# A conditioned attention and token-mixing block on one core: the same operations in a new issue order, with other engines for some norms and evacuations

## The chip, the cores and the metric

One core of a Trainium2 chip runs the whole program. The metric is the device time of one execution in microseconds (us). The core has five engines that run their own instruction lists in order and wait for each other through semaphores: TensorE (PE; its weight loads are listed apart as PEld), VectorE (DVE), ScalarE (ACT), GpSimd (POOL) and SyncE (SP). SP does no arithmetic here; it issues nearly all transfers (DMAs), one after the other.

## What is computed

```
h = layernorm(x) * (1 + ca) + sa                      # x: 2048 x 512
x = x + ga * A(h, wqkv, wo)
h = layernorm(x) * (1 + cb) + sb
x = x + gb * B(h, w1, b1, w2, b2)                     # sa..gb: six rows of silu(c) @ w_mod

A: q, k, v = h @ wqkv   (32 heads of 16)
   each position attends to 8 positions: itself and 2, 4, .. 14 back
   softmax over the 8, weighted sum of v, then @ wo
B: h = layernorm(h);  u = gelu(h^T @ w1 + b1)         # over the 2048 positions: 512 x 1792
   y = u @ w2 + b2;   return y^T
```

All inputs and the output are bf16. There are three layernorms per position: two on x and one inside B.

## The kernel before

The 2048 positions are 16 tiles of 128 (`st` 0 to 15), in five chunks of 2, 4, 4, 4 and 2 tiles. A chunk has 256 or 512 columns once it is transposed.

Each chunk goes through the same steps; their names are the tokens of the issue order:

- `ln1s`, `rstd1`, `nb1`, `n1`: the first layernorm. The statistics of a tile are a pair of VectorE instructions (for tiles 10 to 13 two ACT passes and `ln1v`), `rstd` two tiny ACT functions, `nb` one tiny VectorE instruction for the tiles of a group, and `n1_<tile>` the norm itself, one 128x512 instruction. A norm can run on ACT, VectorE or GpSimd.
- `tr`/`hT` (chunks 0 and 1: transposes on TensorE, copied out of PSUM) or `xt` (chunks 2 to 4: transposing DMAs).
- `wsc`: the three weight blocks of the projection, scaled once by 1 + ca, in four pieces each.
- `qkv<chunk>_<t><j>`, `ev...`: projections for q, k and v (t = 0, 1, 2) and their evacuation from PSUM with a bias.
- `qk<chunk>_<i>`, `red`: VectorE multiplies q with the 8 shifted copies of k, for a quarter of the head's lanes at a time, into one of four `big` buffers (a "full product" has 128x4096 elements, a "half" one, in chunks 0 and 4, 128x2048); TensorE sums it over lanes into the logits in `psL`.
- `max`, `sub`, `exp`, `esum`, `rcp`, `smB`: the softmax, going between VectorE, TensorE and ACT.
- `a2`, `vd`: DMAs that lay the weights and the shifted v out for the next step. `pv`, `pvacc`, `oev`: the weighted sum, with four products per chunk on VectorE like those of `qk`, summed on TensorE.
- `wo`, `x1`, `ln2q`: output projection, residual, and the sums for the second layernorm. `ln2m`, `rstd2`, `nb2`, `n2`: that layernorm. `aff`: times 1 + cb plus sb, two VectorE instructions. `ln3s`, `rstd3`, `nb3`, `h3`: the third layernorm.

The first product of B (`mlp1`) sums over positions. It is cut in three sweeps, so that its first part can run when only the first tiles are normed: `mlp1_<sweep>_<f>_<tile>` are 128x512 matmuls from that tile on; `park` puts a partial sum into SBUF, `inj` puts it back by an identity matmul, `padd` adds it on VectorE; `gelu` follows on ACT. The second product (`mlp2_<tile>`) has 14 matmuls per output tile; `fin` (two VectorE instructions) finishes a tile and `st_out` stores it. The last tile is done in pieces of 256, 128 and 128 columns. Loads of weights are `ld_...`, on SP's queue in the order of their tokens.

Nothing on the device schedules. The string `ORDER` (L182 to L238) lists all operations; `_Graph.schedule` (L85) takes them in that order, gives each its buffer from a pool (six PSUM banks `ps`, four `big`, five `vd`) and each engine issues its own in that sequence. A suffix selects the engine where several are possible (`:a` ACT, `:d` VectorE, `:p` GpSimd), and `:q` makes a matmul four 32-column ones (`mm`, L511). For the norms the engine comes from the tuple `NE` (L265: one string per layernorm, one letter per tile), and `ln_norm` (L404) hands only that one on. Where a group's norms are all on VectorE, `nb` is left out (L397).

Idle stretches of TensorE are filled by matmuls of the identity with itself: `fill:2:70` and `fill:4:16` (70 and 16, `fill_fn`, L517) and four `warm` of 9 (L522). They read `ident`, which GpSimd builds (`mk_ident`, L463).

All instructions are recorded by one helper, so each line of the profile says L133; operations are told apart by tile names: `psS` is a PSUM bank, `psL` the logits, `h` any of the normed tiles, `wst` streamed weights, `m` the maxima, `lsb` the softmax weights, `gT` the values after gelu or a parked partial sum.

Of the kernel before, what the change touches and what calls it, by code (L numbers as in the profile page):

```python
# [41 lines left out]
class _Graph:  # L42
# [42 lines left out]
    def schedule(self):  # L85
# [4 lines left out]
        for pos, token in enumerate(ORDER.split()):  # L90
            name, *rest = token.split(":")
            if name == "fill":
                k, n = map(int, rest)
                f = _Op(-1, [("pe", 0.06 * n, lambda k=k, n=n: self.fill_fn(k, n))], 0.0, "filler", 0)
                f.alloc = f.frees = f.behind = None
                order.append(f)
                continue
# [85 lines left out]
consts ld_x_1_2 act_table ld_x0 ld_x_1_4 ld_c ld_x_2_8 ld_x1 ident ld_x_2_6 ld_wmod1 ln1s3 halo0 ld_wqkv1 cps  # L183
ln1s2 warm2 ld_wqkv0 silu_exp ld_wmod0 ln1s0 ln1s4 ln1s1 ln1s5 rstd1_0 ld_x_4_14 nb1_0 ln1s9 rstd1_1 n1_0 n1_1
silu_dve nb1_1 ld_wqkv2 ln1s8 fill:2:70 tr0_0 n1_2 n1_4 modcols1 ln1s7 hT0_3:a n1_5 n1_3 ld_x_3_10 hT0_2:d a1col
hT0_0:a fill:4:16 tr1_2 wsc1_2:d ld_b1 hT0_1:a wsc1_3:d wsc1_0:a tr1_0 wsc1_1:d ln1s6 hT1_2:a ld_wmod2 qkv0_10
ld_x_3_12 wsc0_0:d rstd1_2 wsc0_1:d qkv0_12 wsc0_2:d hT1_1:a nb1_2 n1_8 n1_9 wsc0_3:d modcols0 hT1_0:d ld_wmod3
hT1_3:a qkv0_00 sab ev0_12:d n1_6 ld_wmod4 qvb0 ln1s14 ld_wo1 qkv0_02 qvb_cp0 ln1s15 ev0_00:a wsc2_2 qvb1
wsc2_0:d qkv1_00 wsc2_3 ev0_10:a ev0_02:d ln1s10 wsc2_1:d qkv1_10 qvb_cp1 qk0_0 ev1_10:a qkv0_22 qk0_1 n1_7
qkv0_20 ln1s13 qk0_2 qkv1_02 xt6 red0_0 ev1_00:a qk0_3 red0_1 red0_2 ev0_22:a ld_wmod5 qkv1_22 qk1_0 ev0_20:a  # L190
qkv1_12 ev1_02:a vd0_1 red0_3 ev1_12:a mask qkv1_11 vd0_0 ln1s11 max0 xt8 qk1_2 qkv1_01 ev1_11:a sub0 qkv1_03
ev1_01:a xt9 exp0 qkv1_13 qk1_1 ev1_03:a xt7 esum0 ev1_13:a qkv1_20 rcp0 vd0_2 ln1s12 qkv1_21 smB0 qk1_3 a2_0_3
modcol2 rstd1_4 qkv1_23 a2_0_0 ev1_22:a a2_0_2 halo_v1:a red1_0 ev1_20:a a2_0_1 red1_1 ln1v10 ln1v12 ln1v11
ln1v13 nb1_4 red1_2 rstd1_3 n1_15 ld_wo3 red1_3 nb1_3 ld_wo2 mcols0 n1_11 n1_10 qkv2_00 max1 ev1_21:a n1_14 xt10
qkv2_02 ev2_00:a pv0_0 qkv2_10 n1_12 ld_wo0 pv0_1 qkv2_11 vd0_3 ev2_10:a ev2_02:a qkv2_12 qk2_0 n1_13 qkv2_01
xt12 ev2_12:a pvacc0_0 ev2_01:a sub1 qk2_2 xt13 qkv2_03 exp1 qkv2_13 xt11 ev2_11:a ev2_03:a qkv2_22 qk2_1
ev2_13:a esum1 ev1_23:a qkv2_21 rcp1 vd1_2 red2_0 smB1 ev2_21:a ld_b2 red2_1 qk2_3 halo_v2:a a2_1_1 red2_2
pvacc0_1 a2_1_3 qkv3_00 a2_1_2 qkv3_10 a2_1_0 pv0_2 mrowt0 vd1_1 qkv2_20 ev3_10:a pv0_3 ev3_00:a red2_3 mrows0:a
qkv2_23 ev2_20:a st_row0 max2 halo_k3:p ev2_22:a vd1_3 qkv3_11 qk3_0 xt14 qkv3_22 ev3_11:a pvacc0_2 ld_row0
pvacc0_3 sub2:q oev0_2:a vd1_0 pv1_2 qkv3_02:q exp2 qkv3_12 ev3_02:a ev2_23:a qkv3_01 pv1_3 oev0_0:a vd2_2 esum2  # L200
modcol3 xt15 rcp2 ev3_12:a woq_s qkv3_20 ev3_01:a pvacc1_3 smB2 ev3_20:a red3_0 qk3_1 ev3_22:a a2_2_0 pvacc1_2
wo1 a2_2_1 vd2_3 qkv3_13:q x1_1 a2_2_2 pv1_1 vd2_1 wo0 ev3_13:a a2_2_3 qkv4_02 ld_w1_0_512 oev1_2:a mcols1 pv1_0
ld_w1_0_0 oev1_3:a mrowt1 qkv3_03 mrows1:a x1_0 st_row1 qkv4_00 ev3_03:a vd2_0 ln2q1 qk3_2 pvacc1_0 ev4_02:a
red3_1 pvacc1_1 oev1_0:a qkv3_23:q oev1_1:a qk3_3 ev4_00:a wo3:q ln2q0 wo5:q pv2_2 qkv4_22:q x1_5 ev3_23:a wo2:q
ld_row1 ln2q5 ld_w1_0_896 ln2m0 halo_v3:a wo4:q x1_3 pv2_1 x1_2 red3_2 x1_4 red3_3 ln2q3 qkv3_21:q pv2_3 rstd2_0
qkv4_20 ln2q2 ev3_21:a ev4_22:a vd3_3 pvacc2_1 nb2_0 max3 pvacc2_2 n2_0 warm0 ln2q4 vd3_0 n2_1 ln2m2 sub3 pv2_0
pvacc2_3 oev2_2:a exp3 rstd2_2 esum3 oev2_1:a aff0 pvacc2_0 rcp3 oev2_0:a qkv4_10 oev2_3:a ln2m4 nb2_2 smB3
warm3 n2_2 ev4_10:a ln3s0 wo6 a2_3_0 n2_3 ln3s1 a2_3_1 rstd2_4 wo7 x1_6 vd3_1 aff2 rstd3_0 a2_3_2 biascols wo9:q
ev4_20:a a2_3_3 nb2_4 nb3_0 ln3s3 n2_5 n2_4 vd3_2 warm1 ln3s2 h3_1 h3_0 qkv4_12 aff4 rstd3_2 wo8 x1_7 ld_w2_0
nb3_2 ln3s5 h3_3 h3_2 ln2q6 ln3s4 mlp1_0_6_0 ev4_12:a pv3_0 mlp1_0_3_0 x1_9 rstd3_4 mlp1_0_5_0 x1_8 mlp1_0_0_0  # L210
biascols_cp:a ln2q8 nb3_4 pv3_1 halo_v4:a mlp1_0_2_0 h3_4 vd4_1 h3_5 mlp1_0_1_0 ln2q9 pv3_2 ld_w2_1 mlp1_0_2_4
vd4_2 ln2q7 mlp1_0_0_4 vd4_0 mlp1_0_3_4 park0_0:a mlp1_0_1_4 mlp1_0_5_4:q park0_1:a ln2m6 vd4_3 pv3_3 park0_2:a
pvacc3_0 pvacc3_1 oev3_0:a ld_w1_0_1152 pvacc3_2 oev3_1:a mlp1_0_4_0:q rstd2_6 oev3_2:a qk4_2 pvacc3_3 park0_3:a
mlp1_0_7_0 oev3_3:a nb2_6 qk4_1 n2_6 mlp1_0_6_4 mlp1_0_4_4 n2_8 qk4_0 wo12:q ld_w1_0_1408 n2_7 n2_9 qk4_3 wo10:q
park0_4:a aff6 x1_12 red4_0 wo13:q ld_w2_3 park0_5:a ln2q12 red4_1 red4_2 x1_10 red4_3 wo11:q max4 ln2q10 ln3s9
x1_13 sub4:q mlp1_0_8_0:q exp4 ln3s8 ln2q13 mlp1_0_11_0 esum4 ln3s7 rcp4 mlp1_0_12_0 park0_6:a ln3s6 x1_11
mlp1_0_10_0 smB4 rstd3_6 ln2m12 a2_4_2 mlp1_0_9_0 h3_7 rstd2_12 h3_6 a2_4_3 ln2q11 h3_9 mlp1_0_8_4 ln2m13 a2_4_0
nb2_12 ln2m11 n2_12 mlp1_0_7_4 a2_4_1 ln2m10 h3_8 rstd2_10 ld_w2_4 aff12 mlp1_0_9_4 rstd2_13 rstd2_11 nb2_10
ln3s12 mlp1_0_9_8 mlp1_0_7_8 n2_10 mlp1_0_8_8 nb2_13 pv4_0 park0_7:a mlp1_0_12_4 ld_w1_0_1664 park0_8:a
mlp1_0_11_4 nb2_11 pv4_2 n2_13 mlp1_0_10_4 rstd3_12 pv4_1 park0_9:a mlp1_0_12_8 n2_11 mlp1_0_10_8 pv4_3 inj1_4  # L220
mlp1_0_11_8 ld_w1_1_0 park0_10:a pvacc4_2 ld_w1_1_640 park0_11:a pvacc4_0 nb3_12 aff11 pvacc4_1 h3_12 pvacc4_3
mlp1_0_13_0 aff10 oev4_0:a oev4_2:a aff13 mlp1_0_13_4 ln3s10 wo15 ld_w2_5 ln3s13 rstd3_10 mlp1_0_13_8 wo14 x1_15
rstd3_13 park0_12:a inj1_0 nb3_13 ln2s15 mlp1_1_0_6 nb3_10 x1_14 rstd2_15 mlp1_1_4_6 park0_13:a nb2_15 ln2s14
n2_15 inj1_3 inj1_6 ld_w1_1_896 inj1_5 mlp1_1_6_6 rstd2_14 aff15 h3_10 mlp1_1_3_6 ln3s15 mlp1_1_6_10 ln3s11
mlp1_1_0_10 rstd3_15 inj1_1 mlp1_1_1_6 park1_0:a nb3_15 h3_15 n2_14 rstd3_11 aff14 mlp1_1_5_6 h3_13 ln3s14
mlp1_1_5_10 mlp1_1_1_10 inj1_2 ld_w1_2_0 mlp1_1_2_6 h3_11 rstd3_14 park1_1:a h3_14 mlp1_1_4_10 mlp1_1_3_10
mlp1_1_2_10 mlp1_1_9_10 park1_2:a ld_w1_1_1408 park1_3:d mlp1_1_7_10 padd1_9 park1_4:a park1_5:d mlp1_1_8_10
padd1_7 gelu7 mlp1_1_10_10 park1_6:a mlp1_2_2_11 ld_w1_2_640 padd1_10 mlp1_2_2_14 mlp1_2_0_11 padd2_2
mlp1_2_0_14 ld_w2_7 gelu2 mlp1_2_1_11 padd2_0 mlp1_2_1_14 gelu0 mlp1_1_12_10 padd2_1 gelu10 padd1_8 gelu1
mlp1_2_5_11 gelu8 mlp1_2_5_14 gelu9 mlp1_2_6_11 mlp1_2_3_11 padd2_6 mlp1_2_3_14 ld_w2_9 mlp1_2_4_11 padd2_3  # L230
# [11 lines left out]
def kernel(  # L242
# [10 lines left out]
    c: bass.AP,  # L253
    w_mod: bass.AP,
    out: bass.AP,
    SIZES=(2, 4, 4, 4, 2),
    MIX=((0, 7, (6, 11)), (7, 14, (10,))),
    NPRE=6,
    NBIG=4,
    NVD: int = 5,  # L260
    NHT: int = 2,
    NA2: int = 2,
    NB=2,
    NH2=2,
    NE=('PAPAAPAADAAPAAPD', 'PAPAAPAAAADAAADP', 'APPAAADDDDADAADA'),  # L265
    X1D=(14, 15),
    ESD=(4,),
    LN1A=(10, 11, 12, 13),
    LN2D=(14, 15),
    GRP=(2, 2, 4, 1, 1),  # L270
    XDMA=(2, 3, 4),
    INJ=(1,),
    WARM=4,
    VPOOL=(2, 3),
):
    nc = _OrderedNC(tc, 1)
    G = _Graph(dict(ps=6, big=NBIG, vd=NVD))
# [109 lines left out]
    def ln_rstd(l, g0, n, name, var=None, vreads=None):  # L387
# [9 lines left out]
        if vreads is None and NE[l][g0:g0 + n] == "D" * n:  # L397
            return
# [118 lines left out]
    def fill_fn(k, n):  # L517
        for _ in range(n):
            nc.tensor.matmul(psS[k][:, 0:P], lhsT=ident[:], rhs=ident[:], start=True, stop=True)
# [519 lines left out]
```

## Time and profile before

| | |
|---|---|
| median of 3 runs | 206.48 us (206.46 to 206.7) |
| span of the profiled execution, first to last instruction | 204.6 us |
| TensorE busy | 194.7 us (95%), 1655 matmuls |
| VectorE busy | 163.3 us (80%), 260 instructions |
| ACT busy | 120.6 us (59%), 283 |
| GpSimd busy | 13.0 us (6%), 36 |
| norms on ACT, 128x512 | 27, mean 0.805 us |
| norms on VectorE, 128x512 | 10, mean 0.404 us |
| norms on GpSimd, 128x512 | 11, mean 0.806 us |
| weighted products on VectorE, 128x4096 | 24, mean 2.285 us |
| moved by DMA | 35.93 MB, mean 176 GB/s |

The span is what the trace covers; 1.9 us lie around it. Busy times of engines overlap and don't add up to the span. A matmul's listed duration (379 ns for 512 columns) covers its whole way through the array; the next one starts about 213 ns later. In the lists of instructions a line reads: start, duration, engine, source line, operation, output<-input, shape, count; neighbours of the same kind are merged, with their count.

### The profile page before, as it was taken

The numbers are of one execution on the slowest core, as the hardware profiler recorded it, in microseconds if no ns is written. First come the engines' busy times: TensorE is split into PE (matmuls) and PEld (weight loads), VectorE is DVE, ScalarE is ACT, GpSimd is POOL, SyncE is SP. The second block draws the span as 40 slices with busy tenths as digits, with TensorE's granted clock in tenths as the row PEclk, the third lists the DMA queues.
The fourth block names the chain that finished last, engine by engine and source line by source line (L and its number), as shares of the span: only waits on it lengthen the run. The fifth ranks groups of instructions, "written<-read, shape, count | busy, mean of one in ns | idle before, by whom it ended". The sixth has DMA issues, their size and how long they took to land.

```text
span 204.6 us, 4223 instructions
## 1 busy us (share of the span) xinstructions
PE 194.7 (95%) x1655; PEld 103.5 (51%) x1655; DVE 163.3 (80%) x260; ACT 120.6 (59%) x283; POOL 13.0 (6%) x36
## 2 busy tenths in 40 slices
PE   3999999999999997989899999999999999999994
PEld 3988554454455553554344445444444444444453
DVE  2899999999999999999999999975473204369365
ACT  2398998994666899989898876683762000000000
POOL 4122001100000001240000000100000000000000
PEclk9999999999999999999999999999999999999999
DMA  5999494646958976194975179946990930121121
GB/s 141 330 380 348 117 239 107 161 98 201 247 186 267 308 234 251 25 272 110 289 200 115 26 157 263 288 131 200 340 304 3 232 88 16 39 77 51 51 82 51
DMA packets 55111, 35.93 MB, mean 176 GB/s; under 512 B 24628, under 2 KB 52404, under 8 KB 55092
## 3 DMA queue, kind: packets, MB, share of 16 engines
q1 hardware_dynamic: 55084, 35.67, 61.4%
q8 instruction: 13, 0.21, 0.4%
q14 instruction: 6, 0.05, 0.1%
q10 hardware_dynamic: 8, 0.00, 0.0%
HBM read 22.55 MB, written 2.10 MB: 121 GB/s over the span
## 4 chain that ended last, share of the span: by engine, by line
PE 65%; DVE 20%; issue 5%; DMA 5%; SPq 3%; ACT 2%; DVEq 0%
PE psS L133 62%; DVE big L133 9%; DVE h L133 3%; PE psL L133 3%; SPq L133 3%; DVE st L133 3%; DMA wst<-in_B_w_dram 2%; DMA xx<-in_A_x_dram 2%; ACT h L133 1%; DVE mv L133 1%; DVE m L133 1%; DVE lsb L133 1%; DVE ls L133 0%; DVE nb L133 0%; DVE woq L133 0%
## 5 line engine op out<-in xcount | busy, mean ns | idle before, releaser
L133 PE MATMUL psS<-h,wst 128*128 128x512 bf16 (+1 forms) x254 | 50.7, 379 | 1.2 <-POOL h L133 0.7
L133 PE MATMUL psS<-hT,w_qkv 128*128 128x512 bf16 (+3 forms) x312 | 46.2, 339 | 0.3 <-ACT w_qkv L133 0.3
L133 PEld LDWEIGHTS <-wst 128*128 128x128 bf16 (+1 forms) x356 | 28.7, 98 | 32.2 <-issue 3.2
L133 PEld LDWEIGHTS <-w_qkv 128*128 128x128 bf16 (+1 forms) x354 | 29.5, 111 | 21.3 <-issue 3.2
L133 DVE TENSOR_TENSOR big<-a2sb,vD 128x4096 bf16<-128x4096 bf16 (+1 forms) x20 | 36.9, 1876 | 0.0
L133 DVE TENSOR_TENSOR big<-q_sb,k_f 128x4096 bf16<-128x4096 bf16 (+1 forms) x20 | 36.3, 1857 | 0.0
L133 DVE SCALAR_TENSOR_TENSOR h<-psS,bcol,rows_bc 128x512 f32<-128x512 f32 (+2 forms) x18 | 12.4, 690 | 24.4 <-PE psS L133 24.2
L133 PE MATMUL psS<-gT,big 128*128 128x512 bf16 x112 | 24.8, 379 | 0.0
L133 PEld LDWEIGHTS <-big 128*128 128x128 bf16 x144 | 12.0, 97 | 13.2
L133 PEld LDWEIGHTS <-ident 128*128 128x128 bf16 (+1 forms) x203 | 13.9, 111 | 5.9 <-issue 2.8
L133 PE MATMUL psS<-woq,o_sb 128*32 128x512 bf16 (+1 forms) x172 | 16.6, 380 | 0.0
L133 ACT ACTIVATE h<-xx,nb,rs 128x512 bf16<-128x512 bf16 x19 | 15.0, 807 | 0.8 <-DVE nb L133 0.7
L133 DVE TENSOR_TENSOR psS<-psS,gT 128x512 f32<-128x512 f32 x14 | 9.3, 696 | 7.0 <-PE psS L133 7.0
L133 ACT ACTIVATE junk<-xx 128x512 bf16<-128x512 bf16 x22 | 13.8, 626 | 0.2
L133 POOL TENSOR_SCALAR h<-xx,rs,nb 128x512 bf16<-128x512 bf16 x9 | 7.3, 813 | 101.3 <-DVE nb L133 84.0
L133 ACT ACTIVATE lv<-mv,epscol 128x1 f32<-128x1 f32 (+2 forms) x25 | 7.3, 291 | 9.3 <-DVE mv L133 8.4
L133 DVE BATCH_NORM_STATS2 st<-xx 128x6 f32<-128x512 bf16 x14 | 9.5, 678 | 4.0 <-DMA xx<-in_A_x_dram 4.0
L133 ACT ACTIVATE gT<-psS,bcol 128x512 bf16<-128x512 f32 x14 | 8.7, 688 | 6.4 <-DVE psS L133 6.4
L133 PEld LDWEIGHTS <-group 128*32 128x32 bf16 x288 | 6.8, 96 | 10.2 <-issue 4.8
L133 DVE TENSOR_TENSOR h<-h,rows_bc 128x512 bf16<-128x512 bf16 (+2 forms) x20 | 11.5, 581 | 0.5
L133 DVE TENSOR_TENSOR h<-h,xx 128x512 bf16<-128x512 f32 (+2 forms) x18 | 11.4, 633 | 0.6
L133 ACT ACTIVATE gT<-psS 128x512 bf16<-128x512 f32 x19 | 10.8, 587 | 1.6 <-PE psS L133 1.5
(94 smaller groups left out, 220.4 us busy)
## 6 DMA issues: line engine op xcount, KB each, us to landing
vD<-v_sb SPq DMA_DIRECT2D x12, 524.5 KB, 3.8
big<-in_B_w_dram SPq DMA_DIRECT2D x4, 896.0 KB, 8.2
vD<-v_sb SPq DMA_DIRECT2D x8, 268.5 KB, 3.0
wst<-in_B_w_dram SPq DMA_DIRECT2D x3, 640.0 KB, 5.3
out_dram<-h SPq DMA_DIRECT2D x15, 128.0 KB, 1.8
xx<-in_A_x_dram SPq DMA_DIRECT2D x7, 256.0 KB, 6.1
wst<-in_B_w_dram SPq DMA_DIRECT2D x2, 800.0 KB, 4.8
gT<-in_w_mod_dram SPq DMA_DIRECT2D x3, 512.0 KB, 6.1
```

Of the source, the lines that this page charges most:

```text
L133: r = fn(*a, **k)
```

## The change

The operations are the same but for a few fills and column operations. The string `ORDER` is new as a whole. The rest of the diff, nearly complete:

```diff
         for pos, token in enumerate(ORDER.split()):
             name, *rest = token.split(":")
-            if name == "fill":
-                k, n = map(int, rest)
-                f = _Op(-1, [("pe", 0.06 * n, lambda k=k, n=n: self.fill_fn(k, n))], 0.0, "filler", 0)
...
-    NE=('PAPAAPAADAAPAAPD', 'PAPAAPAAAADAAADP', 'APPAAADDDDADAADA'),
...
-    WARM=4,
+    WARM=(9, 70, 16),
...
-        if vreads is None and NE[l][g0:g0 + n] == "D" * n:
-            return
...
-    def ln_norm(l, g0, n, st, dst, src, reads, writes, name, by_sums=False):
...
+    def ln_norm(l, g0, st, dst, src, reads, writes, name):
+        rs, nb = ln_t["rs", l], ln_t["nb", l]
+        r_, n_ = rs[:, st, 0:1], nb[:, st, 0:1]
+        G.add_any([("act", 0.8, lambda: nc.scalar.activation(dst, src, ACT.Identity, scale=r_, bias=n_)),
+                   ("dve", 0.42, lambda: nc.vector.tensor_scalar(dst, src, r_, n_, op0=ALU.mult, op1=ALU.add)),
+                   ("pool", 0.8, lambda: nc.gpsimd.tensor_scalar(dst, src, r_, n_, op0=ALU.mult, op1=ALU.add))],
+                  reads=reads + [("rs", l, g0), ("nb", l, g0)], writes=writes, name=name, locks=True)
...
-    for w_ in range(WARM):
+    for w_, n_w in enumerate(WARM):
         s_w = _Slot("ps")
 
-        def f_warm(s_w=s_w):
-            for _ in range(9):
+        def f_warm(s_w=s_w, n_w=n_w):
+            for _ in range(n_w):
                 nc.tensor.matmul(ps(s_w)[:, 0:P], lhsT=ident[:], rhs=ident[:], start=True, stop=True)
```

Every `nb` is now computed, and the engine of a norm is its suffix in `ORDER` (ACT where there is none). Two stretches of the old and the new order, at the start and (new order alone) where the third norm of tiles 4 and 5 and the second of tiles 6 and 7 stand:

```diff
-consts ld_x_1_2 act_table ld_x0 ld_x_1_4 ld_c ld_x_2_8 ld_x1 ident ld_x_2_6 ld_wmod1 ln1s3 halo0 ld_wqkv1 cps
-ln1s2 warm2 ld_wqkv0 silu_exp ld_wmod0 ln1s0 ln1s4 ln1s1 ln1s5 rstd1_0 ld_x_4_14 nb1_0 ln1s9 rstd1_1 n1_0 n1_1
-silu_dve nb1_1 ld_wqkv2 ln1s8 fill:2:70 tr0_0 n1_2 n1_4 modcols1 ln1s7 hT0_3:a n1_5 n1_3 ld_x_3_10 hT0_2:d a1col
-hT0_0:a fill:4:16 tr1_2 wsc1_2:d ld_b1 hT0_1:a wsc1_3:d wsc1_0:a tr1_0 wsc1_1:d ln1s6 hT1_2:a ld_wmod2 qkv0_10
+ld_x_1_2 ident warm1 ln1s3 ld_x0 ld_x1 ld_c ln1s0 ln1s1 ld_x_1_4 act_table ld_wqkv1 ln1s4 rstd1_0 nb1_0 n1_0:a cps
+ln1s2 ld_wmod1 ln1s5 n1_1:p tr0_0 ld_x_2_6 silu_exp silu_dve rstd1_1 hT0_2:d nb1_1 n1_4:p hT0_1:d ld_wmod0 halo0
+hT0_3:a n1_3:d ld_wqkv0 n1_5:a modcols1 a1col wsc1_2:a n1_2:d tr1_2 wsc1_1:a ld_x_2_8 hT1_3:a ld_b1 tr1_0 hT1_1:a
+wsc1_3:d hT1_0:a wsc0_1:a hT0_0:d wsc0_0:a ld_x_4_14 wsc1_0:d qkv0_10 consts ev0_10:a ln1s6 ld_wqkv2 wsc2_2 ln1s7
...
+nb3_4 a2_3_1 h3_4:p h3_5:p x1_8 mlp1_0_5_0 a2_3_0 a2_3_2 pv3_2 ln2q9 ln2q8 ln2m6 rstd2_6 vd3_1 mlp1_0_0_0
+halo_v4:a pv3_0 mlp1_0_1_4 mlp1_0_3_4 mlp1_0_0_4 nb2_6 n2_6:p park0_0:a park0_1:a n2_8:a mlp1_0_2_4 park0_2:a
+mlp1_0_4_4 mlp1_0_6_0 mlp1_0_6_4 park0_3:a pvacc3_2 n2_7:p mlp1_0_5_4 oev3_2:a pv3_1 mlp1_0_8_0 pvacc3_1
```

What the orders say by count:

| | before | after |
|---|---|---|
| norms on ACT / VectorE / GpSimd | 27 / 10 / 11 | 13 / 9 / 26 |
| n1 on GpSimd (tiles) | 0, 2, 5, 11, 14 | 1, 4, 7, 8, 9, 10, 11, 14, 15 |
| n2 on GpSimd | 0, 2, 5, 15 | 1 to 7, 9, 13, 15 |
| h3 on GpSimd | 1, 2 | 0, 3, 4, 5, 8, 9, 10 |
| weight scalings on ACT / VectorE / GpSimd | 1 / 9 / 2 | 6 / 4 / 2 |
| hT copies on VectorE | 2 of 8 | 3 of 8 |
| ev and park on VectorE | 4 | 0 |
| small halo copies on GpSimd | 1 | 3 |
| identity matmuls: ahead of the first projection / in the middle | 95 / 27 | 70 / 25 |
| mlp1 matmuls ahead of sub4 in TensorE's order | 46 | 74 |
| mlp1 and inj matmuls split in columns (:q) | 10 | 64 |

In the new order `fin14` and four stores stand ahead of the last two pieces of tile 15, whose 256 columns come earlier; `mlp2` starts with tile 7; tile 0, whose matmuls stand in three parts, comes eighth and no longer first.

## The prediction

> **What bounds the kernel now.** I read the busy rows in slices first, then the busy time by stage, then the chain of waits, and last the order of time on VectorE, GpSimd and TensorE.
>
> ```profile
> PE   3999999999999997989899999999999999999994
> DVE  2899999999999999999999999975473204369365
> POOL 4122001100000001240000000100000000000000
> ```
>
> TensorE (PE) and VectorE (DVE) are both full from the third slice to the twenty-sixth; from there on only TensorE is. GpSimd (POOL) is nearly empty. A "full" PE can hide waits, so the stages come next (us, busy time and count for PE, PEld, DVE, ACT, POOL, then granted clock, DMA share, GB/s):
>
> ```profile
> 20.00:30.00 10.00, 10.00 (x71) 5.57 (x70) 10.00 (x8) 9.57 (x23) 0.00 (x0) 1.00 0.75 197
> 80.00:90.00 10.00, 9.21 (x96) 5.46 (x95) 9.72 (x21) 9.31 (x24) 2.67 (x3) 1.00 0.50 169
> 100.00:109.20 9.20, 8.46 (x128) 3.74 (x121) 9.17 (x10) 8.52 (x21) 0.00 (x0) 1.00 0.92 246
> 144.00:201.60 57.60, 57.57 (x295) 27.50 (x293) 29.14 (x44) 7.67 (x13) 0.00 (x0) 1.00 0.39 112
> ```
>
> Up to 109 us VectorE hardly rests, while TensorE begins to have holes at 70 us. In the last 57.6 us TensorE has no hole and VectorE is half idle. The chain of waits says where the bound changes hands:
>
> ```profile
> 13.61 9.50 PE psS L133 x108
> ...
> 108.57 0.60 DVE m L133
> ...
> 112.83 88.75 PE psS L133 x465
> ...
> 201.60 0.36 DVE h L133
> ```
>
> So: the first projection starts at 13.61, VectorE leads until the last maximum of the attention logits (max4, started 108.48, 108.48 + 0.68 = 109.16 at its end), then TensorE runs straight to 201.58 and 3.0 us of tail follow. Two quantities make the time: when max4 is done, and how much TensorE work stands behind it (sub4, the matmul that waits for it, started at 109.22).
>
> **The change, step by step.** All is measured against the span of 204.6; the median of 206.48 is 1.9 above it, and I add that at the end.
>
> *Start.* The 70 fill matmuls move to the very front, GpSimd builds the identity first, and the first weight block is issued fifth on SP's queue, not eighth. DVE takes the statistics of tiles 3, 0, 1 first (0.80 each from 3.65, so 6.05), then ACT needs 0.5 for rstd and DVE 0.1 for nb: the norms of chunk 0 start at 7.0 and not 9.2. Following ACT's new list from there (silu, hT0_3, n1_5, two weight scalings at 0.70, three hT1 copies at 0.59, two more scalings, ev0_10, hT1_2, rstd, two halves of ev0_00 at 0.47), the first projection can start at 11.9 and the first attention product (qk0_0) at 17.7, not 19.48. Both are 1.7 to 1.8 earlier. If ACT, which is 89 to 96% busy here, slips, half of this is gone.
>
> *The fills in the middle.* Three groups of 9 in the middle go, a 9 and a 16 stay there: 27 or 25 matmuls at 0.066, no difference. The 16 between the two transposes at 11.2 covered an idle PE; they are worth nothing unless the clock falls back (a rival below).
>
> *TensorE work.* From the first projection on it is the same set. I count 128x512 matmuls at 0.213 (8 us hold 37.5 of them at the end). A change between full and column-split matmuls costs 0.11: four full ones take 0.87, but before a split one the next start comes 0.97 later:
>
> ```profile
> 58.33 1.04 PE L133 MATMUL psS<-hT,w_qkv 128*128 128x512 bf16 x4
> 59.30 0.61 PE L133 MATMUL psS<-big,group 128*32 128x512 bf16 x8
> ```
>
> There are 34 such changes before and 38 after: 0.4 more, with the new ":q" marks counted. Up to sub4 the work is 87.2 + 31 x 0.11 = 90.6 before and 93.0 + 37 x 0.11 = 97.1 after; behind sub4 it is 89.8 and 83.8. So 6.0 us of MLP matmuls move from behind max4 to before it, where TensorE has holes: a gain of 6.0, if max4 does not come later.
>
> *VectorE up to max4.* Start to start, from the order of time: a full product 2.20, a half one 1.14, a statistics pair 0.78, a norm 0.36. Both kernels do 24 full products (52.8), 12 half ones (13.7), the maxima, scalings and wo scaling (7.9) and the row affine (6.1): 80.4. Column operations: 2.7 before, 3.2 after. Statistics: 6 before, 10 after (4.7, 7.8). Norms: 1 and 2 (0.4, 0.7). Sums 88.2 and 92.2. From 19.48 the old sum ends at 107.7, against 109.16 measured, so 1.5 were lost, 0.35 of it in the collision below. From 17.7 the new one ends at 109.9; with the same 1.1 of idle, 111.0.
>
> *The norms on GpSimd.* This decides. Eleven of the 48 norms run on GpSimd before, 26 after. Before, all but a few stand beside statistics or maxima. Where one met a two-input product, one of the two waited:
>
> ```profile
> 36.01 0.77 POOL L133 TENSOR_SCALAR h<-xx,rs,nb 128x512 bf16<-128x512 bf16 x1
> 36.28 1.57 DVE L133 TENSOR_TENSOR big<-a2sb,vD 128x2048 bf16<-128x2048 bf16 x1
> ...
> 83.77 0.68 DVE L133 TENSOR_TENSOR lsb<-lsb,rb 128x1024 bf16<-128x1024 bf16 x1
> ...
> 83.95 1.15 POOL L133 TENSOR_SCALAR h<-xx,rs,nb 128x512 bf16<-128x512 bf16 x1 [4.48 <-DVE nb L133]
> ...
> 118.32 1.22 DVE L133 TENSOR_TENSOR big<-a2sb,vD 128x2048 bf16<-128x2048 bf16 x1
> ```
>
> The half product took 1.57 beside a norm and 1.22 alone: 0.35 lost, with 0.50 of the norm (36.28 to 36.78) over it. The norm at 83.95 took 1.15, not 0.77, because the product was there first. In the new order 13 norms become ready inside unbroken runs of products before max4: n1_7, n1_9, n1_8 (behind qk0_0), n1_15, n1_10, n1_11, n1_14, n2_1, h3_4, h3_5 and n2_6, n2_7, n2_9. n2_2 to n2_5 stand beside max3 and statistics and cost nothing; h3_0, h3_3, h3_8 and two halo copies meet short operations, 0.3 together. The cost of one: from below 0 (it finds a hole in VectorE's work), from above 0.77 (the whole norm). The nearest row is 0.35 for a partly covered one; a norm that starts when a product ends covers the next one wholly, 0.35 + 0.27 = 0.62. I take the middle, 0.48: 13 x 0.48 + 0.3 = 6.5. The bounds are 0 and 10.3. A norm left on VectorE would cost 0.36, so moving it to GpSimd there buys nothing.
>
> The Trainium skill ("SBUF — State Buffer", Who interferes with whom) speaks against this change: a VectorE instruction with two SBUF inputs and a GpSimd instruction that reads SBUF exclude each other for the whole instruction, and whichever issued first goes on. The two rows above agree with it (1.57 and 1.15). By the letter of that rule each of the 13 would cost the whole 0.77, and the estimate would be 3.8 higher than mine.
>
> The norms that leave ACT (27 at 0.80 before, 13 after) free some 11 us there; five more weight scalings and two more evacuations give 5 back. ACT waits for VectorE in that stage (8.4 us for the statistics), so this buys nothing now; if VectorE were faster, it would.
>
> *From max4 to the end.* max4 ends at 109.9 + 1.1 + 6.5 = 117.5. sub4 is done 0.3 later; 83.8 + 0.1 of TensorE work follow, with the loss that the old kernel had there (201.58 - 109.44 - 89.8 - 0.3 = 2.0): 203.6, against 201.58. VectorE has 21.8 us of work from max4 to the last norm (h3_14) and TensorE 23.6 to the matmul that reads it, so this stays covered, with 2 us to spare.
>
> *Tail.* The last tile's pieces: before 256, 128, 128 columns follow tile 14; after only 128 and 128 (1.5 us of TensorE), so fin14 (0.75 + 0.69) is not done when they end, and its store, tile 13's and the two pieces' queue on SP behind it at 0.4 to 0.65 each. The last issue is done 1.5 to 2.3 after TensorE's end, not 1.06: +0.4 to +1.2, I take 0.7.
>
> *Sum.* 203.6 + 3.0 + 0.7 = 207.3 of span; + 1.9 = 209.2 us. With collisions at nothing it would be 202.7, if TensorE kept up; at 10.3 it is 213.0.
>
> **The rivals.**
>
> *A: the norms cost VectorE nothing and the earlier start carries through (faster).* For it: 11 us less on ACT, the earlier start, 6.0 us of MLP work drawn forward. Against it: the 1.57. TensorE then leads: 11.9 + 97.1 = 109.0 at sub4, plus the 5.0 it lost in that stretch before (109.22 - 13.6 - 90.6) = 114.0, + 83.9 + 1.9 = 199.8, + 3.7 + 1.9 = 205.4; if it loses less, down to the 202.7 above. It decides when all collisions together stay under 3.8 us (0.27 each). Expected 204.8.
>
> *B: the clock falls back at the start (slower than my forecast).* Counts of matmuls in one microsecond:
>
> ```profile
> 8.00:9.00 1.00, 1.00 (x12) 1.00 1.06 353
> ...
> 10.00:11.00 1.00, 1.00 (x25) 1.00 1.09 387
> ```
>
> The fills ran at half pace for their first 5.5 us (3.19 to 8.7). In the new order they end near 8.3 and PE has about 2 us of work in the 3.6 us to the first projection. If the pace halves once more, 3.4 us of projections take 6.8, ACT's pace hides 1 to 1.5, qk0_0 slips by 2: 211.2.
>
> The skill ("TensorE: Matmul & The Clock Gate", Part 1) puts the gate at about 3.4 us of idle; the new gap is shorter than that and not idle throughout, so by it the pace would hold. No run here has shown a fall back yet.
>
> *C: it does little.* The collisions come to 0.27 each and eat the gain: 206.5.
>
> **How the numbers follow.** My forecast 0.60, A 0.20, B 0.12, C 0.08. What a measurement here can tell from no change is about 0.2%, 0.4 us. Faster: A and a fifth of C, 0.22. Same: 0.05. Slower: the rest, 0.73. The range goes from the middle of A (203.5) to my case at the upper bound of the collisions (213.5); the forecast's own range is 207.0 to 213.0.
>
> **What would show it.** Right: products beside GpSimd norms at 2.6 to 3.0 and not 2.28, norms over 0.77, GpSimd busy some 25 us, max4 ending after 115, qk0_0 at 17 to 18.5, TensorE unbroken behind sub4. Wrong: products at 2.28 throughout, max4 before 114, or TensorE waiting for something other than VectorE in the middle (transposed tiles of chunk 2, which need n1_8 and n1_9 from GpSimd, would be the first to come late), or projections at 12 us at half pace.

## The result

| | before | after |
|---|---|---|
| median | 206.59 us | 222.57 us (220.03, 225.68, 220.87, 224.28) |
| ratio, 95% interval | | 1.066 [1.062, 1.070] |
| span of the profiled execution | 204.6 us | 218.0 us |

Two of the four runs (225.68 and 224.28) had TensorE's clock at 0.959 and 0.958 and not 0.976; such slow runs are in the medians, here and below, and not in the ratios, and the profile is of the 220.03 run. The change makes the kernel 6.6% slower. The forecast was 209.2 with 213.5 as its upper bound: the direction was right, the size far too small.

The busy rows of the changed kernel, in 40 slices:

```profile
DVE  3889995999099899998996998988465004796464
POOL 1337990009303100145593130610000000000000
PEclk9969996999988999999999999999999999999999
```

VectorE now has holes where it had none (slices 7, 11 and 22, of 5.45 us each), GpSimd is busy in many stretches (53.8 us, 13.0 before), and the granted clock falls three times. Cut at the ends of the five maxima, the stages read as follows (window, length, then busy time and count of PE, PEld, DVE, ACT, POOL, then granted clock, DMA share, GB/s); first three of the old kernel's stages, then all of the new kernel's:

```profile
36.40:51.80 15.40, 15.40 (x113) 7.37 (x112) 15.40 (x11) 11.39 (x22) 0.91 (x2) 1.00 0.57 163
...
79.70:109.16 29.46, 27.24 (x289) 13.54 (x289) 28.85 (x44) 27.75 (x71) 3.45 (x4) 1.00 0.72 197
109.16:201.60 92.44, 91.89 (x497) 43.11 (x492) 58.98 (x120) 32.13 (x75) 0.77 (x1) 1.00 0.48 133
```

```profile
18.28:26.70 8.42, 8.33 (x143) 5.24 (x144) 8.42 (x10) 8.34 (x19) 8.42 (x5) 1.00 0.80 236
26.70:40.80 14.10, 11.53 (x90) 5.18 (x89) 11.56 (x11) 9.66 (x26) 5.86 (x2) 0.88 0.60 155
40.80:63.20 22.40, 17.48 (x184) 9.21 (x185) 16.99 (x17) 14.15 (x31) 7.78 (x5) 1.00 0.45 137
63.20:92.90 29.70, 29.19 (x228) 15.05 (x231) 28.44 (x24) 21.55 (x51) 3.98 (x4) 0.94 0.61 190
92.90:126.90 34.00, 30.29 (x213) 13.66 (x216) 30.68 (x49) 24.23 (x69) 17.62 (x12) 1.00 0.69 179
126.90:214.25 87.35, 85.45 (x606) 41.34 (x608) 54.40 (x107) 27.55 (x62) 5.33 (x3) 1.00 0.47 132
```

The old maxima ended at 26.9, 36.4, 51.8, 79.7 and 109.16. From the first product to max4 VectorE was busy 88.8 of 89.7 us before and 96.1 of 108.6 after. With the start, the stretch behind max4 and the tail, the 13.4 us of span add up:

| | before | after | difference |
|---|---|---|---|
| first product (qk0_0) | 19.48 | 18.28 | -1.2 |
| VectorE's work up to max4 | 88.8 | 96.1 | +7.3 |
| VectorE idle up to max4 | 0.9 | 12.5 | +11.7 |
| max4 to TensorE's end | 92.4 | 87.35 | -5.1 |
| tail | 3.0 | 3.75 | +0.75 |

The largest term is idle time on the engine that sets the pace. In VectorE's order of time the brackets give the idle time ahead of an instruction and what ended it:

```profile
37.37 2.29 DVE L127 TENSOR_TENSOR big<-q_sb,k_f 128x4096 bf16<-128x4096 bf16 x1 [2.54 <-ACT q_sb L127]
59.75 2.29 DVE L127 TENSOR_TENSOR big<-a2sb,vD 128x4096 bf16<-128x4096 bf16 x1 [5.38 <-DMA a2sb<-lsb]
...
116.50 2.49 DVE L127 TENSOR_TENSOR h<-h,rows_bc 128x2048 bf16<-128x2048 bf16 x2 [2.02 <-POOL h L127]
```

The middle one has its origin 11 us earlier, and the chain of waits names it:

```profile
48.66 3.29 POOL h L127
...
54.56 0.78 POOL h L127
55.34 0.50 SPq L127
55.89 0.58 SPq L127
56.52 3.01 DMA a2sb<-lsb
59.75 2.29 DVE big L127
```

Tile norms on GpSimd, and the VectorE instructions beside the one that starts at 48.66 (n1_10):

```profile
L127 POOL TENSOR_SCALAR h<-xx,rs,nb x19: 768/772/5918, 7.5 to 145.8; 128x512 bf16<-128x512 bf16 x19
...
48.47 1.22 DVE L127 TENSOR_TENSOR big<-a2sb,vD 128x2048 bf16<-128x2048 bf16 x1
49.61 4.49 DVE L127 TENSOR_TENSOR big<-q_sb,k_f 128x4096 bf16<-128x4096 bf16 x2
54.01 0.16 DVE L127 CAST mcols<-psS 128x12 bf16<-128x12 f32 x1
```

Minimum, median and maximum of a norm are 768, 772 and 5918 ns. The longest one is this: it starts beside three products that follow each other without a gap, none of them is lengthened (1.22, and 4.49 for two), and it ends only when a small copy out of PSUM comes at 54.01. VectorE loses nothing there. The norm does, and with it `xt10`, which waits for it at the head of SP's queue until 54.6, and `a2_1_2`, which has nothing to do with that norm but stands two places behind `xt10` in the queue. VectorE then stands still for 5.4 us, waiting for `a2_1_2`.

### The profile page after: what moved, and what is told of

Same layout as the page of the kernel before. It is cut to its first block, busy times and chain, and to the rows that moved or that the text cites. A ratio compares the mean times of both kernels' runs of the same rounds, so it can differ in the third digit from the quotient of the medians.

```text
span 218.0 us, 4211 instructions
## 1 busy us (share of the span) xinstructions
PE 196.9 (90%) x1631; PEld 102.7 (47%) x1649; DVE 164.4 (75%) x255; ACT 115.9 (53%) x276; POOL 53.8 (25%) x53
## 4 chain that ended last, share of the span: by engine, by line
PE 49%; DVE 18%; issue 9%; DMA 7%; POOL 6%; ACT 6%; SPq 3%; DVEq 0%; POOLq 0%; ACTq 0%
PE psS L127 48%; DVE big L127 8%; POOL h L127 6%; DVE h L127 3%; DMA a2sb<-lsb 3%; SPq L127 3%; DVE st L127 2%; DMA hT<-h 2%; DMA xx<-in_A_x_dram 2%; DVE mv L127 2%; ACT q_sb L127 1%; PE psL L127 1%; ACT o_sb L127 1%; DVE m L127 1%; ACT w_qkv L127 1%
## 5 line engine op out<-in xcount | busy, mean ns | idle before, releaser
L127 PE MATMUL psS<-h,wst 128*32 128x512 bf16 (+1 forms) x400 | 50.7, 379 | 3.7 <-POOL h L127 2.7
L127 PE MATMUL psS<-hT,w_qkv 128*128 128x512 bf16 (+3 forms) x305 | 49.6, 346 | 3.1 <-issue 2.6
L127 POOL TENSOR_SCALAR h<-xx,rs,nb 128x512 bf16<-128x512 bf16 x19 | 34.3, 1815 | 58.8 <-DVE nb L127 57.8
L127 PEld LDWEIGHTS <-wst 128*128 128x128 bf16 (+1 forms) x506 | 29.8, 98 | 33.8 <-issue 5.0
L127 DVE TENSOR_TENSOR big<-q_sb,k_f 128x4096 bf16<-128x4096 bf16 (+1 forms) x20 | 38.3, 1936 | 3.4 <-ACT q_sb L127 2.5
L127 PEld LDWEIGHTS <-big 128*128 128x128 bf16 x144 | 12.1, 99 | 13.9 <-DMA big<-in_w_mod_dram 0.8
L127 POOL TENSOR_SCALAR h<-h,rs,nb 128x512 bf16<-128x512 bf16 x7 | 12.0, 1727 | 18.7 <-DVE nb L127 18.5
L127 PE MATMUL psS<-woq,o_sb 128*128 128x512 bf16 x61 | 15.9, 379 | 0.2 <-issue 0.2
L127 PEld LDWEIGHTS <-ident 128*128 128x128 bf16 (+1 forms) x161 | 11.8, 112 | 5.4 <-POOL epscol L127 1.4
L127 DVE TENSOR_TENSOR h<-h,xx 128x512 bf16<-128x512 f32 (+2 forms) x18 | 11.4, 633 | 3.4 <-DMA out_dram<-h 2.8
L127 ACT ACTIVATE q_sb<-psS,qvb 128x512 bf16<-128x512 f32 (+1 forms) x20 | 11.3, 596 | 2.8 <-PE psS L127 2.8
L127 ACT ACTIVATE k_f<-psS 128x512 bf16<-128x512 f32 x16 | 9.2, 594 | 5.3 <-PE psS L127 5.2
```

Of the source, the lines that this page charges most:

```text
L127: r = fn(*a, **k)
```

## The experiments

All are ratios to runs of the kernel before on the same chip (medians 206.7 to 207.3). Maxima are given where they matter, from the profiles. A profile is of one run; those of x5, x6 and x11 are of runs of 226.66, 222.87 and 218.16 us.

**The engine of the norms, first look.**

```diff
 x1: n1_7, n1_9, n1_10, n1_11, n1_14, n2_1.. h3_4.. : ":p" -> ":a" or the old engine; n1_8:d, n1_15:d; places as they are
 x2 (old kernel), eleven more norms on GpSimd:
-    NE=('PAPAAPAADAAPAAPD', 'PAPAAPAAAADAAADP', 'APPAAADDDDADAADA'),
+    NE=('PAPAAPAPPPPPAAPP', 'PPPAAPPPAPDAAADP', 'APPAPPDDDDADAADA'),
 x3: a2_1_2 moved ahead of xt10
 x4: as x1, but the first layernorm alone
```

> The new order as it is, but no norm on GpSimd from tile 6 of the first layernorm on (they go to ACT, or to VectorE where the old kernel had them there). Theory T (norms on GpSimd are held off by VectorE's products, and what waits for them stalls the rest): the two long gaps of VectorE (2.5 us near 35, 5.4 near 55) go, max4 ends near 112, the time is 204 to 209 us. Rival R (the new order is slow in itself, by its DMA queue and its softmax chains): the gaps stay and the time is over 214.

> The old order as it is, with 11 more norms on GpSimd among the products (n1 of tiles 7, 8, 9, 10, 15; n2 of 1, 6, 7, 9; h3 of 4, 5). Theory T: norms of 2 to 6 us instead of 0.77, and 5 to 13 us more than the old kernel (211 to 220). Rival R: the old order keeps its time within 2 us.

> The new order, with one DMA (a2_1_2, the last piece of chunk 1's softmax weights) issued ahead of the transposing DMA xt10 that waits for the late norm of tile 10. If the queue behind xt10 is what VectorE's 5.4 us near 55 are made of: that gap falls under 1 us and the time by 3 to 5 us (215 to 217). If the late norm holds more than this queue: the next step waits instead, and the time changes by less than 1.5 us.

> The new order, with only the seven first-layernorm norms from tile 6 on taken off GpSimd (19 stay in all). Theory T with the early norms as its main part: both long gaps go, 207 to 212 us. If the later norms (n2, h3) are the main part: 215 to 219 us.

| | median | ratio |
|---|---|---|
| x1 | 227.28 | 1.096 [1.092, 1.099] |
| x2 | 215.47 | 1.040 [1.035, 1.045] |
| x3 | 224.57 | 1.083 [1.077, 1.088] |
| x4 | 224.79 | 1.081 [1.075, 1.087] |

x2 shows that norms on GpSimd can cost 8 us by themselves, in the old order. Its maxima end at 26.4, 36.1, 51.9, 79.8 and 117.3: the early norms cost nothing, all is lost in the last stage. GpSimd, TensorE and VectorE there:

```profile
95.08 7.71 POOL L133 TENSOR_SCALAR h<-h,rs,nb 128x512 bf16<-128x512 bf16 x2 [3.21 <-DVE nb L133]
...
100.00 0.58 PE L133 MATMUL psS<-h,wst 128*128 128x512 bf16 x1 [3.17 <-POOL h L133]
102.85 3.76 PE L133 MATMUL psS<-h,wst 128*128 128x512 bf16 x15 [2.27 <-POOL h L133]
...
106.89 1.23 DVE L133 TENSOR_TENSOR big<-q_sb,k_f 128x2048 bf16<-128x2048 bf16 x1 [4.73 <-PE psS L133]
```

Two norms (h3_4, h3_5) take 7.71 us and not 1.54. The `mlp1` matmuls of these tiles wait 5.4 us, the attention's work behind them in TensorE's queue waits with them, and VectorE, whose products held the norms up, then waits 4.7 us for TensorE.

x1 and x4 were meant to take this away in the new order and were slower than it. They have a flaw: n1_8 stands late in the new order, a place made for GpSimd, whose queue is short, and on VectorE it is late (VectorE waits 5.5 us in x1 and 5.8 in x4 for chunk 2's `q_sb`). x3 removes the 5.4 us wait (max2 at 58.2 and not 63.2), and other waits of 5.9, 3.0 and 1.9 us come behind it; its time is no lower (1.083).

**The same with n1_8 and n1_10 early, the clock, the tail.**

```diff
 x5: x1, and
-nb1_2 n1_7:p .. qk0_1 ev1_11:a n1_9:p n1_6:a .. rcp0 red1_0 n1_8:p xt8 .. nb1_3 n1_15:p n1_10:p
+nb1_2 n1_8:d n1_7:a .. qk0_1 ev1_11:a n1_9:a n1_6:a .. rcp0 red1_0 xt8 .. nb1_3 n1_10:d n1_15:d
 x6: x5's first layernorm alone
 x7: fills: 8 behind tr0_0, 12 behind modcols1, 30 ahead of qkv2_10, 65 (not 9) ahead of sub2
 x8: the old end: .. mlp2_12_0 .. mlp2_14_0 mlp2_15_0 fin14_0 mlp2_15_1 st_out14_0 fin15_0 mlp2_15_2 ..
```

> The new order with no norm on GpSimd from tile 6 of the first layer norm on, as in x1_no_pool_norms, but n1_8 now stands right behind nb1_2 and n1_10 right behind nb1_3, both on VectorE, so that the transposes of chunk 2 are not held up by a late place in an in-order queue. Theory T (what is lost comes from the norms on GpSimd, and x1 missed it only because n1_8 stood late): 205 to 211 us, the wait of VectorE for q_sb near 41 us gone, max4 ended before 116. Rival O (the order itself keeps too little TensorE work in reserve, whatever engine does the norms): 216 or more, with waits of VectorE for q_sb or of TensorE for evacuations in other places. 211 to 216: both have a share.

> As x5_no_pool_norms_early for the first layer norm only (tiles 6 to 15 off GpSimd, n1_8 and n1_10 early); the norms of the second and third layer norm stay on GpSimd as in the changed kernel. If T holds, it lies between x5 and the changed kernel and tells the early norms from the late ones: early ones cost most (they gate transposes): within 2 us of x5; late ones cost most: within 2 us of the changed kernel's 220. By O it is no better than 218.

> The changed kernel with fill matmuls in the four places where TensorE was idle ahead of a stretch at half clock: 8 and 12 around the column products at 8 to 11 us, 30 ahead of the first projection of chunk 2 (31 to 33 us), 65 and not 9 ahead of sub2 (59 to 63 us). Nothing else moves. Rival B (the clock that falls back is a large part of the loss): the granted clock goes from 0.976 to over 0.99 and the time falls by 3 us or more. Theory T: VectorE sets the pace there, so that the clock rises and the time moves by less than 1.5 us (218.5 to 221.5).

> The changed kernel with the old end: tile 14, then the three pieces of tile 15 (256, 128, 128 columns) as the last TensorE work, stores in the order in which they become ready. The tail behind the last matmul goes from 5.3 us back to 3.0 to 3.7, everything up to 212 us stays: 1.5 to 2.3 us less, about 218. If the tail comes from the transfers themselves (nine stores at the end, whatever their order), it stays above 4.7.

| | median | ratio |
|---|---|---|
| x5 | 223.39 | 1.079 [1.074, 1.084] |
| x6 | 220.88 | 1.065 [1.057, 1.073] |
| x7 | 221.36 | 1.067 [1.059, 1.074] |
| x8 | 220.83 | 1.065 [1.059, 1.071] |

x5 refutes the theory that the norms on GpSimd are the whole cause: no norm from tile 6 on runs there, the longest wait for `a2sb` shrinks from 5.4 to 0.8 us, and the time does not fall (1.079 against 1.066). Now TensorE waits 7.0 us for the same norms from ACT, where they stand behind ACT's other work.

x7 shows what the clock is worth. Around the first projections, in the changed kernel and then in x7:

```profile
10.00:11.00 1.00, 0.11 (x5) 0.02 (x1) 1.00 (x5) 0.89 (x2) 1.00 (x3) 1.00 1.08 382
...
14.00:15.00 1.00, 1.00 (x15) 0.74 (x13) 0.71 (x2) 1.00 (x3) 0.00 (x0) 0.50 1.11 337
```

```profile
10.00:11.00 1.00, 0.78 (x14) 0.59 (x11) 1.00 (x5) 1.00 (x3) 1.00 (x4) 1.00 1.10 387
...
14.00:15.00 1.00, 1.00 (x22) 0.99 (x21) 0.97 (x3) 1.00 (x3) 0.00 (x0) 1.00 1.11 335
```

With 20 fills the clock stays whole at 14 us (1.00, not 0.50) and qk0_0 starts at 17.01 and not 18.28. Of these 1.3 us the clock made 1.1: from the first projection to qk0_0 it is 6.30 us in the changed kernel and 5.22 in x7, as in x12 and x13 below, which have the same fills; the first projection itself was 0.2 earlier in x7. The maxima end 0.9, 3.0, 2.9 and 3.6 us earlier: 25.8, 37.8, 60.3, 89.3. Then max4 ends at 127.2, no earlier than without fills:

```profile
100.03 7.79 POOL L127 TENSOR_SCALAR h<-h,rs,nb 128x512 bf16<-128x512 bf16 x2 [3.63 <-DVE nb L127]
...
107.87 5.05 PE L127 MATMUL psS<-h,wst 128*128 128x512 bf16 x15 [4.59 <-POOL h L127]
...
113.52 2.29 DVE L127 TENSOR_TENSOR big<-a2sb,vD 128x4096 bf16<-128x4096 bf16 x1 [6.18 <-PE psS L127]
```

The same two norms as in x2. In the changed kernel they took 3.55 us together and cost TensorE 1.1; in x7, x3, x4 and x6 VectorE waited 5.9 to 7.3 us at this place. So some 3 us gained up to max3 were given back to another wait, and the time is that of the changed kernel (1.067 against 1.066).

x8 gives a tail of 3.0 us and not 3.75, a gain of 0.75, too little to show in its time (1.065 against 1.066). The 5.3 us in its expectation was a misreading: the last matmul of the changed kernel ends at 214.25.

**Halves of the two orders.** Both orders hold the same operations, so a prefix of one can be followed by the rest of the other.

```diff
 h1: new order up to qk0_0 (not included), then the old     h2: new up to max1, then the old
 h3: new order up to max2, then the old                     h4: old up to max2, then the new
```

> A hybrid: all operations that stand ahead of qk0_0 in the new order, in that order and on those engines; behind them the rest in the old order and on the old engines. Theory E (the changed kernel loses in its middle; its start is better than the old one): the first product at 18.3 and not 19.5, and 205 to 206.2 us, faster than before. Rival: the earlier start is worth nothing, because chunk 2's buffer of transposed tiles and the transfers set the pace behind it: 206.5 or more.

> As h1, but cut behind max1: the new order up to the second chunk's maximum (36.4 us in the old kernel, 40.8 in the changed one), the old order behind it. If what is lost by then stays lost: about 4 us over before, 210 to 212. If the late maximum is made up later, since other VectorE work was done ahead of it: 206 to 208.

> Cut behind max2, which ends at 51.8 us in the old kernel and at 63.2 in the changed one. Theory E (the loss arises up to max2: late transposed tiles of chunk 2, then a2_1_2 behind xt10 in the queue): 212 to 218. Rival L (the loss arises behind max2, where the norms of the later layer norms on GpSimd hold up the MLP matmuls, which stand ahead of the attention's in TensorE's queue): 210 or less.

> The reverse: old order and engines up to max2, the new order and its engines behind it. By E: 206 to 210, the 6.6 us shorter stretch behind max4 showing as a gain. By L: 212 or more. If both halves cost, h3 and h4 together come to about 14 to 16 over before (13.5 to 16 is what the changed kernel loses).

| | median | ratio | ends of the maxima |
|---|---|---|---|
| h1 | 208.17 | 1.007 [1.004, 1.010] | 27.9, 37.3, 52.8, 80.6, 110.1 |
| h2 | 214.44 | 1.035 [1.029, 1.041] | 27.8, 39.5, 59.0, 86.8, 116.3 |
| h3 | 221.58 | 1.067 [1.060, 1.074] | 27.5, 41.1, 63.5, 94.0, 123.5 |
| h4 | 222.96 | 1.077 [1.073, 1.081] | 28.1, 37.5, 53.0, 90.9, 129.9 |

The earlier start brings nothing in h1: the first projection runs at 12.1, but small VectorE operations of the old order come between, and qk0_0 starts at 19.44. What is late at max1 in h2 is later still at max2 and stays lost. Each half of the new order costs as much as the whole, so the losses do not add. Part of each is its seam, the place where the two orders meet: at 57 us h4 waits 4.4 us for a load that the old half had not yet issued, and at 69 us h3 waits 5.4 us for the next chunk's `q_sb`, a wait that the changed kernel does not have. How much of the losses the seams are was not tested.

**The norms in each half, and both together.**

```diff
 h6: h4 with
-nb3_4 a2_3_1 h3_4:p h3_5:p .. nb2_6 n2_6:p .. n2_8:a .. n2_7:p .. n2_9:p .. n2_1:p .. h3_8:p .. h3_9:p
+nb3_4 h3_4:d h3_5:d a2_3_1 .. nb2_6 n2_6:d n2_7:d n2_9:a .. n2_8:a .. n2_1:a .. h3_8:a .. h3_9:a
 h7: h3 with x5's edit      x11: the new order with both edits
 x9: NHT 2 -> 3 (a third buffer of transposed tiles), nothing else
 x12: x11 with x7's fills of 8, 12, 30      x13: the new order with h6's edit and all of x7's fills
```

> h4_old_to_max2 with the late norms off GpSimd: h3_4, h3_5, n2_6, n2_7 on VectorE and n2_9 on ACT, each right behind its nb, n2_1, h3_8, h3_9 on ACT in their places. Theory G (in the late half it is the norms on GpSimd, which keep the MLP matmuls, and the attention's behind them in TensorE's queue, waiting): TensorE's 6.1 us of waits for GpSimd and VectorE's 7.4 us behind them go, 222.9 falls to 213 to 217. Rival O (the order): TensorE waits for the same norms from another engine, 220 or more.

> h3_new_to_max2 with the norms of tiles 6 to 15 of the first layer norm off GpSimd, n1_8 and n1_10 on VectorE right behind their nb. Theory G: the wait for a2sb (5.5 us, a2_1_2 queued behind xt10, which waits for n1_10) and most of those for q_sb (8.2) go, and 221.6 falls to 209 to 213. Rival O: the wait for a2sb goes, those for q_sb stay, 216 or more.

> The whole new order with both edits (early norms as in x5 and h7, late ones as in h6). By G in both halves: 206 to 212. By O: 217 or more. If the late half is G and the early one O, as I now hold: 213 to 217, max2 near 61 and 64 to 67 us from there to max4.

> The changed kernel with three buffers for the transposed tiles and not two, so that the transposes of chunk 2 (first issue at 22.57) wait for their norms alone and not for the last projection of chunk 0. If the buffer is what holds chunk 2 up: first transpose ahead of 21.5, VectorE's 2.54 us wait for q_sb at 37 gone, max1 at 38 to 39 and not 40.8, and the time lower by up to 3. If the norms on GpSimd hold it up: the first transpose earlier, the last (25.27 + 5.76) not, max1 at 40 or later.

> x11_both_off_pool with the fills of x7 around 8 to 11 us and ahead of chunk 2's first projection (8, 12 and 30 matmuls; the 65 ahead of sub2 are left out, TensorE is not idle there in x11). If the half-clock stretches explain x11's spread: clock over 0.99 in all runs, first product near 17.0, and 211 to 214, in all runs within 1%. What then remains over the old kernel's 206.6 to 207 is the order alone. If fills only fill: 217 to 219 as x11.

> The changed kernel with the late norms off GpSimd as in h6 and x11 and all the fills of x7 (8, 12, 30, 65); the early norms (tiles 7 to 15 of the first layer norm) stay on GpSimd. If the early ones cost what max2 showed between x11 and the changed kernel (59.6 against 63.2): 2 to 4 us over x12, 214 to 217, with max2 near 60 as in x7, and no wait of VectorE for TensorE over 2 us ahead of max4. If they cost nothing once the clock holds: within 1.5 us of x12.

| | median | ratio |
|---|---|---|
| h6 | 218.86 | 1.057 [1.051, 1.062] |
| h7 | 216.38 | 1.043 [1.035, 1.051] |
| x11 | 218.17 (one run 213.80) | none |
| x9 | 222.38 | 1.061 [1.055, 1.067] |
| x12 | 217.82 | 1.054 [1.049, 1.058] |
| x13 | 220.14 | 1.063 [1.056, 1.070] |

Off GpSimd and early, the norms are worth 4.1 us in the late half (h4 to h6; VectorE's wait for TensorE goes from 7.4 to 1.9) and 5.0 in the early one (h3 to h7, by the ratios; the wait for `a2sb` goes from 5.5 to 1.0). Neither fell as far as expected. In the whole new order less is left of it: by the ratios x12 lies 1.2% (2.5 us) below the changed kernel, fills included, and x13 against x12 puts 1.9 us on the early norms (by the ratios; it is near the noise, and x13 has 56 more fills in the middle). x9 moves the first transpose of chunk 2 from 22.57 to 21.75 and leaves max1 at 40.4: the buffer is not what holds chunk 2 up. x11's single run at 213.8 had the clock at 0.992, the others at 0.968 to 0.975; x12 held the clock (0.980 to 0.992) and did not reach it, so the fills themselves, or other timing, take back what the clock gives. That is not settled.

What is left in x12, where GpSimd still does six norms up to max4 but the longest pair takes 2.25 us and the clock is mostly whole (VectorE from its first product to max4, then its longer waits):

```profile
18.04:123.45 105.41, 97.24 (x883) 48.98 (x885) 96.58 (x114) 82.58 (x201) 11.31 (x10) 0.98 0.69 181
...
36.11 2.29 DVE L127 TENSOR_TENSOR big<-q_sb,k_f 128x4096 bf16<-128x4096 bf16 x1 [1.61 <-ACT q_sb L127]
55.96 2.29 DVE L127 TENSOR_TENSOR big<-a2sb,vD 128x4096 bf16<-128x4096 bf16 x1 [2.16 <-DMA a2sb<-lsb]
75.00 4.49 DVE L127 TENSOR_TENSOR big<-a2sb,vD 128x4096 bf16<-128x4096 bf16 x2 [1.35 <-DMA a2sb<-lsb]
110.12 2.29 DVE L127 TENSOR_TENSOR big<-a2sb,vD 128x4096 bf16<-128x4096 bf16 x1 [1.66 <-PE psS L127]
```

VectorE works 96.6 us there, 7.8 more than in the old kernel, and still idles 8.8, 8.0 more, in many small waits with different causes. Not all of the 7.8 is the order: nine norms stand on VectorE in this stretch and one in the old kernel, which is 2.4 us, and seven of the nine were moved there by x12's own edit. Another 2.4 us are four more statistics ahead of max4. VectorE's first product starts 1.4 earlier, and x12 gets 4.7 back behind max4 (87.75), with 1.0 more of tail: 7.8 + 8.0 - 1.4 - 4.7 + 1.0 = 10.7, and 215.2 - 204.6 = 10.6.

One of these waits can be followed to the order itself. Chunk 2's transposes on SP's queue and TensorE's work after them, in the old kernel and then in the changed one:

```profile
26.69 3.93 SPq L133 DMA_TRANSPOSE hT<-h  x3
...
33.16 1.91 PE L133 MATMUL psL<-big,group 128*32 128x512 bf16 x32
35.01 5.37 PE L133 MATMUL psS<-hT,w_qkv 128*128 128x512 bf16 x24
```

```profile
25.27 5.76 SPq L127 DMA_TRANSPOSE hT<-h  x3
...
33.01 1.58 PE L127 MATMUL psS<-hT,w_qkv 128*128 128x512 bf16 x3 [2.37 <-issue]
```

The transposes leave SP's queue at about the same time in both (30.6 and 31.0); in the changed kernel the last one lands at 32.9, just ahead of the 33.01. In the old order every red1 and qkv1_20, 21 and 23 stand ahead of the first projection of chunk 2, which therefore never waits. The new order puts qkv2_10 ahead of qkv1_20 to 23, red1_2 and red1_3: TensorE stands idle for 2.4 us in front of work that it could do, and goes on at half clock. The norms on GpSimd do not make this gap: in x11 and x5, where no norm of chunk 2 runs there, the last transpose lands at 33.2 and 33.4, and TensorE stands idle for 2.37 and 2.34 us. VectorE's 2.54 us at 37.4 follow, and most of them come from the half clock: x7, whose 30 fills fill the gap, keeps the clock at 1.00 here and VectorE's wait is 0.42. An order with qkv2_10 behind these was not tried.

## Why the prediction was too low

- **Start.** First projection at 11.98 (11.9 foretold), qk0_0 at 18.28 (17.7). Half right: rival B's fall of the clock did happen at the start and cost 1.1 us by x7, where B had 2.
- **Middle fills.** Priced at nothing unless the clock fell back. It fell back, so the proviso held; x7's fills, which stand in four other places, are worth 3 us up to max3 and nothing at the end.
- **TensorE behind max4.** 87.35 us measured, 86.1 foretold (203.6 - 117.5). The gain from MLP work drawn forward is 5.1 and not 6.3: a size slightly off.
- **VectorE's work.** 92.2 + 6.5 = 98.7 foretold with collisions, 96.1 measured. The sum is near by luck. Start to start, the products total 68.6 us against 66.9 before, 1.7 more, where 13 norms were to cost 6.5. The column operations took 5.1 (3.2 foretold) and the two norms 1.0 (0.7); a few of these stood beside a norm on GpSimd and were lengthened too (column operations of 0.55 and 0.48 us, 0.16 alone).
- **"With the same 1.1 of idle, 111.0".** This step failed: the idle time was carried over from the old kernel without a reason. VectorE idled 12.5 us up to max4. Three waits are 9.9 of it: 5.4 for `a2_1_2`, which stood behind n1_10's transpose in SP's queue, 2.5 for chunk 2's `q_sb`, and 2.0 for norms on GpSimd (116.50). The forecast put max4 at 117.5 and it came at 126.9: 9.4 late, of which 11.4 is idle time, 0.6 the later start, and -2.6 the work.
- **"The norms on GpSimd. This decides."** It looked at the right pair of engines and priced the wrong one. A collision cost VectorE 0.43 (a half product took 1.65, not 1.22), close to the 0.48 taken. But a norm that meets a run of products waits up to 5.1 us itself, and what waits for it (transposes, and everything behind them on SP's in-order queue; `mlp1` matmuls, and the attention behind them on TensorE's) was given no price. The last paragraph of the prediction named the transposed tiles of chunk 2 as what would be late first. TensorE did wait 2.4 us for them, though not because of GpSimd; n1_10 and its neighbour in the queue cost more (5.4).
- **Tail.** 3.75, 3.7 foretold: right. x8 confirms it (3.0 with the old end).
- **Signs.** Of those for "right", max4 came after 115 and qk0_0 within 17 to 18.5, but GpSimd was busy 53.8 us and not some 25: the norms waited there. Of those for "wrong", two came: TensorE waited for chunk 2's tiles, and the first projections ran at half clock.
- **Rivals.** A and C did not happen. B did, but as a side term.

What the runs show of the size: the engine of the norms is 8 us in the old order, 4 to 5 in each half of the new one, 2 to 3 in the whole (one run of x11, at 213.8, would make it more). About 11 us are left in x12: 8 us more of VectorE's work ahead of max4, 2.4 of it norms that moved to VectorE, for 5 us less behind it, and 8 more of idle time. That this rest is the order is argued from what remains and not shown by a run that mends it; the cause of most of it stays open. Which tokens make the scattered waits was not followed one by one. No version here beats the old kernel.

## What to carry to other kernels

An engine that is nearly idle is not free: ask how long an operation waits there beside the engine that sets the pace, and what stands behind it in every in-order queue that its result gates. When a pacing engine shows hardly a gap in 90 us (0.9 us here), do not carry its idle time over to a new order as if it were a constant: here it became 12.5. Work moved ahead of it is paid at once (7.3 us), and the gain behind it (5.1) comes only if no new waits arise. A wait that was removed alone came back as another one (x3, x5, x7), so judge a fix by the end of the stage, not by the wait.

## What was not expected of the hardware

- A GpSimd norm beside back-to-back two-input products on VectorE waited through several of them: 0.77 us alone, up to 5.9 beside them, 7.7 for two. The Trainium skill ("SBUF — State Buffer", Who interferes with whom) says that whichever was issued first holds the shared ports for the whole instruction and the other blocks; the traces agree with the exclusion, and show that between products that follow without a gap the waiting GpSimd instruction often does not get its turn (49.61 to 54.01 above), though sometimes it does (19.48, a product of 1.65).
- The granted clock went to 0.50 at 13 us, after TensorE had been busy 0.62, 0.44 and 0.11 of the microseconds from 8 to 11 us, then 0.98 and 0.78. The Trainium skill ("TensorE: Matmul & The Clock Gate", Part 1) gives an idle window of about 3.4 us; here no idle stretch ahead of it was over 0.9 us, so the forecast's reading, that the pace would hold, was wrong. A light load does not always bring the fall: in h1, whose list is the same up to qk0_0, the shares were 0.93, 0.39 and 0.22, the gaps 0.6 and 0.9 us, and the clock stayed at 1.00. What decides between the two is not shown; with 20 fills it stayed whole in x7, x12 and x13.
